# Rows s and -s in one partition block: an FFT mixing and channel-mix kernel on Trainium2

## The chip, the cores and the metric

The kernel runs on one core of a Trainium2 chip. The metric is the device time of one execution in microseconds (us). A core has engines that run side by side, each with a queue of its own in program order: TensorE (PE in the profile; PEld is its weight load), VectorE (DVE), ScalarE (ACT), GpSimd (POOL) and SyncE (SP). POOL also issues the loads that convert float32 to float16, SP the stores.

## The reference

```python
X = np.fft.fft(np.fft.fft(x, axis=1), axis=2).real     # x: 8 x 3072 x 256, float32
X_prev = X shifted by one row along axis 1, zeros first
xk = mu_k * X + (1 - mu_k) * X_prev
xr = mu_r * X + (1 - mu_r) * X_prev
k = np.maximum(xk @ w_k, 0)                             # 256 -> 1024
v = (k * k) @ w_v                                       # 1024 -> 256
out = 1 / (1 + np.exp(-(xr @ w_r))) * v                 # float32
```

## The kernel before

An image is one of the 8 batch entries. The FFT over 3072 rows is split as 48 x 64: row n = 64 n1 + s, with n1 from 0 to 47 and s from 0 to 63. Three stages of matrix products make the real part of the spectrum.

Stage A sums over n1. A load puts 96 partitions of x into SBUF as float16 (`xh`, in two halves h of 16 columns q each): partition p holds the rows 32 p to 32 p + 31, so the even partitions hold s = q and the odd ones s = q + 32. `butterfly` (line 117) adds and subtracts the two halves of the features into `eo`; then `a_item` (line 438) multiplies eight 96 x 128 blocks, as weights, with the table `w_pm` of 96 moving columns (48 parts of frequencies times the two values of s in a block). For image 0 and half of image 1, `a_sum` (line 452) works on `xh` itself, with two accumulating products of 192 columns in place of a butterfly and two of 96. `evac` (lines 424 and 426) copies PSUM to `a` in float16, on DVE ("V") or ACT.

Stage D transforms the features. For each of 24 units u, the weights are a 128 x 128 block of `a` (the real and the imaginary part of a frequency times 64 values of s) and the moving matrix is `w_eo` of 128 columns, 64 cosine and 64 sine; e = 0 and 1 are the even and odd features (`d_units`, line 462). Four units make a `d_item`, evacuated to `g_all` with 1024 elements a partition. Cosine and sine columns are formed for all 128 rows of a block.

Stage C sums over s. `c_item` (line 493) takes for each of 27 slots (a frequency each, from -1 to 25) two blocks of `g_all` as weights, with the tables `m1` and `m2` of 64 columns as moving matrices, into `pq`. Feature 128 doesn't fit into the 128 partitions: image 0 has a third product a slot for it, the others form it with `turned` (three small DVE products, line 509), two products at the end of the last item (line 499), a small evacuation `f` and a small store within SBUF (`flat`, line 516).

Then `halves` (line 525), `diff` and `mix` on DVE give the mixed inputs, and the main loop runs 48 chunks of 512 rows (six an image) of four steps each: `k_piece` (wk, line 589; its Relu on ACT, line 599), `square` on DVE (line 606), `r_item` (wr, line 613; Sigmoid on ACT, line 618), `v_tile` (wv, line 627) and `v_out` (line 637; stores, line 645).

The order is written by hand: `pin_order` at the end holds each engine to program order. What belongs to later images stands in a table of steps, filled by `at(step, f, ...)`: in each step PE gets a `k_piece`, then due items of A, D, C and r, then a `v_tile`. While the chunks of image b run, stages A, D and C of image b + 2 are fed in between, and DVE forms the inputs of image b + 1. PSUM tiles come from three slots of 1024 columns (`ps_w`, used by A, D, C, k and r in turn) and two of 512 (`ps_v`). The x of image b + 3 is loaded when a buffer of `xh` (two) comes free.

Ahead of the loop stands the prologue (lines 649 to 677): POOL issues the loads of image 0 and 1 and the weights' gathers, with small operations between them; DVE and ACT make the tables `w_pm`, `w_eo`, `m1` and `m2` from index patterns and sines; PE runs stage A of image 0 as x arrives, and its first D and C items. `keep_busy` multiplies zeros.

Of the kernel before, what the change touches and what calls it, by code (L numbers as in the profile page):

```python
# [17 lines left out]
MAGIC = 12582912.0  # L18
# [15 lines left out]

@with_exitstack
def kernel(
# [17 lines left out]
    GU = 386  # L54
    NS1 = 17

    const = ctx.enter_context(tc.tile_pool(name="const", bufs=1))
    xh_pool = ctx.enter_context(tc.tile_pool(name="xh", bufs=2))
# [39 lines left out]
    x_r = x.rearrange("b (p r) d -> b p r d", r=32)  # L98
    xh_t = {}
    eo_t = {}  # L100

    def load_part(b, h, q0, nq):

        nc.gpsimd.dma_start(out=xh_t[b, h][:, q0:q0 + nq],  # L104
                            in_=x_r[b, :, 16 * h + q0:16 * h + q0 + nq, :])
# [46 lines left out]
    def mu_rows(a):  # L152
        for p0, f0, step, n in (((0, 0, 1, 1), (1, 1, 2, 64), (65, 2, 2, 63)),
                                ((0, 128, 1, 1), (1, 255, -2, 64), (65, 254, -2, 63)))[a]:
            nc.scalar.activation(out=mu_p[:, a, p0:p0 + n], in_=_v(mu_row, f0, [(step, n)]),
                                 func=AF.Copy)
# [10 lines left out]
    load_part(0, 0, 0, 8)  # L167
    pcol_i = const.tile([P, 1], INT32)
    nc.gpsimd.iota(pcol_i, pattern=[[0, 1]], base=0, channel_multiplier=1)
    k1c_i = const.tile([P, 24, 2], INT32)  # L170
    nc.gpsimd.iota(k1c_i, pattern=[[1, 24], [0, 2]], base=0, channel_multiplier=0)
    load_part(0, 0, 8, 8)
    veo_i = const.tile([P, 2, 64], INT32)
    nc.gpsimd.iota(veo_i, pattern=[[-1, 2], [2, 64]], base=2, channel_multiplier=0)
# [6 lines left out]
    for c in range(2):  # L181
        nc.gpsimd.tensor_scalar(out=ueo[:, :, c], in0=veo_i, scalar1=pd_f,
                                scalar2=(0.5 + 0.25 * c) * TURN, op0=ALU.mult, op1=ALU.add)
    load_part(0, 1, 0, 4)
    load_part(0, 1, 4, 4)
    kst_i = const.tile([P, NSL + 64], INT32)
    nc.gpsimd.iota(kst_i[:, 0:NSL], pattern=[[1, NSL]], base=-1, channel_multiplier=0)
    nc.gpsimd.iota(kst_i[:, NSL:NSL + 64], pattern=[[1, 64]], base=0, channel_multiplier=0)
    load_part(0, 1, 8, 4)
    load_part(0, 1, 12, 4)  # L190
    for i in range(2):
        nc.gpsimd.tensor_scalar(out=unit[:, i:i + 1], in0=pcol_i[0:2], scalar1=float(i),
                                scalar2=None, op0=ALU.is_equal)
# [3 lines left out]

    phs = {}

    def phase(lo, hi):  # L200
        lo, hi = (lo + 0.5) % 1.0, (hi + 0.5) % 1.0
        if (lo, hi) not in phs:
# [639 lines left out]
```

## Time and profile before

| What | Value |
|---|---|
| median of 14 runs | 455.68 us (454.92 to 458.74) |
| the profiled execution | 457.67 us |
| its span | 455.8 us |
| granted TensorE clock, mean | 0.995 |
| HBM read, written | 28.84 MB, 25.17 MB |

The span is from the first to the last instruction that the profiler records; the execution's own time holds it and what lies around it. Busy times of engines overlap. In the groups of the page and in the timeline a line gives the source line, the engine and the operation, what is written from what, the shape, and how many. Matmuls are pipelined: the busy time of a product includes its way through the array, so the pace of a stage is read from one start to the next. Of the page's costliest groups, these are evacuations (A, r and D):

```profile
L426 ACT ACTIVATE a<-psW 128x768 f16<-128x768 f32 x61 | 49.1, 808 | 3.3 <-PE psW L452 3.3
L618 ACT ACTIVATE r<-psW 128x1024 f16<-128x1024 f32 x48 | 49.0, 1020 | 0.8 <-PE psW L613 0.8
L426 ACT ACTIVATE g_all<-psW 128x1024 f16<-128x1024 f32 (+1 forms) x47 | 47.9, 1027 | 0.0
```

After the bar stand the busy time in us, the mean of one in ns, and, after the second bar, how long the engine stood idle ahead of them and for what.

### The profile page before, as it was taken

The numbers are of one execution on the slowest core, as the hardware profiler recorded it, in microseconds if no ns is written. First come the engines' busy times: TensorE is split into PE (matmuls) and PEld (weight loads), VectorE is DVE, ScalarE is ACT, GpSimd is POOL, SyncE is SP. The second block draws the span as 40 slices with busy tenths as digits, with TensorE's granted clock in tenths as the row PEclk, the third lists the DMA queues.
The fourth block names the chain that finished last, engine by engine and source line by source line (L and its number), as shares of the span: only waits on it lengthen the run. The fifth ranks groups of instructions, "written<-read, shape, count | busy, mean of one in ns | idle before, by whom it ended". The sixth has DMA issues, their size and how long they took to land.

```text
span 455.8 us, 9755 instructions
## 1 busy us (share of the span) xinstructions
PE 445.5 (98%) x4082; PEld 327.7 (72%) x4082; DVE 356.0 (78%) x495; ACT 361.6 (79%) x413; POOL 38.8 (9%) x72
## 2 busy tenths in 40 slices
PE   6999999999999999999999999999999999999995
PEld 3767777777777777777777777777777777666764
DVE  7799879986797868877789777888779755997453
ACT  6899998788788888888887888788878888666661
POOL 5858100000000000000000000000000000000000
PEclk9899999999999999999999999999999999999999
DMA  7865861627521473125622265222222121222223
GB/s 133 123 127 106 181 137 44 132 65 139 118 70 48 81 153 92 47 70 113 142 48 70 61 127 120 66 71 47 71 48 70 46 71 47 71 70 70 70 69 94
DMA packets 32524, 40.25 MB, mean 88 GB/s; under 512 B 3838, under 2 KB 29952, under 8 KB 31232
## 3 DMA queue, kind: packets, MB, share of 16 engines
q1 hardware_dynamic: 27776, 25.07, 21.9%
q0 software_dynamic: 4544, 14.42, 18.7%
q8 instruction: 32, 0.52, 0.5%
q10 hardware_dynamic: 160, 0.13, 0.1%
q14 instruction: 12, 0.10, 0.1%
HBM read 28.84 MB, written 25.17 MB: 118 GB/s over the span
## 4 chain that ended last, share of the span: by engine, by line
PE 93%; ACT 3%; DMA 2%; DVE 1%; issue 1%; POOL 0%; POOLq 0%
PE psV L627 36%; PE psW L589 35%; PE psW L613 9%; PE psW L462 4%; PE psW L438 4%; PE psW L493 3%; DMA xh<-in_x_dram 2%; ACT rl L599 1%; PE psW L452 1%; ACT g_all L426 0%; DVE x L569 0%; ACT L618 0%; ACT a L426 0%; ACT r L618 0%; DVE y L525 0%
## 5 line engine op out<-in xcount | busy, mean ns | idle before, releaser
L599 ACT ACTIVATE rl<-psW 128x1024 f16<-128x1024 f32 x192 | 196.3, 1025 | 79.7 <-PE psW L589 79.4
L627 PE MATMUL psV<-wv_sb,k 128*128 128x256 f16 x1536 | 198.7, 273 | 0.0
L589 PE MATMUL psW<-x,wk 128*128 128x512 f16 (+1 forms) x776 | 196.7, 377 | 0.3 <-ACT rl L599 0.3
L606 DVE TENSOR_TENSOR k<-rl 128x2048 f16<-128x2048 f16 (+1 forms) x98 | 117.5, 1201 | 61.3 <-ACT rl L599 60.6
L627 PEld LDWEIGHTS <-k 128*128 128x128 f16 x1536 | 143.5, 98 | 20.2
L589 PEld LDWEIGHTS <-wk 128*128 128x128 f16 x776 | 75.7, 98 | 50.4 <-issue 0.4
L637 DVE SCALAR_TENSOR_TENSOR o<-psV,r 128x512 f32<-128x512 f32 (+1 forms) x97 | 66.2, 683 | 23.7 <-PE psV L627 21.7
L558 DVE TENSOR_TENSOR x<-y,t 128x1536 f16<-128x1536 f16 x60 | 57.5, 958 | 2.1
L426 ACT ACTIVATE a<-psW 128x768 f16<-128x768 f32 x61 | 49.1, 808 | 3.3 <-PE psW L452 3.3
L613 PE MATMUL psW<-wr,x 128*128 128x256 f16 x384 | 49.8, 273 | 0.0
L618 ACT ACTIVATE r<-psW 128x1024 f16<-128x1024 f32 x48 | 49.0, 1020 | 0.8 <-PE psW L613 0.8
L613 PEld LDWEIGHTS <-x 128*128 128x128 f16 x384 | 37.5, 98 | 14.4
L426 ACT ACTIVATE g_all<-psW 128x1024 f16<-128x1024 f32 (+1 forms) x47 | 47.9, 1027 | 0.0
L117 DVE TENSOR_TENSOR eo<-xh 96x2048 f16<-96x2048 f16 x26 | 31.5, 1213 | 1.6 <-DMA xh<-in_x_dram 1.6
L462 PEld LDWEIGHTS <-a 128*128 128x128 f16 x384 | 25.0, 98 | 10.2 <-issue 0.6
L438 PEld LDWEIGHTS <-eo 96*128 96x128 f16 x416 | 23.4, 97 | 11.6
L104 POOL DMA_DIRECT2D xh<-in_x_dram x21 | 11.2, 537 | 226.0 <-DVE eo L117 221.7
L426 ACT ACTIVATE pq<-psW 128x896 f16<-128x896 f32 (+5 forms) x34 | 28.8, 851 | 0.4 <-PE psW L493 0.3
L462 PE MATMUL psW<-w_eo,a 128*128 128x128 f16 x376 | 28.4, 219 | 0.3 <-ACT rl L599 0.3
L438 PE MATMUL psW<-w_pm,eo 96*128 96x96 f16 x416 | 26.3, 206 | 0.0
L493 PEld LDWEIGHTS <-g_all 128*128 128x128 f16 x459 | 17.8, 98 | 8.3 <-ACT g_all L426 1.7
L493 PE MATMUL psW<-m,g_all 128*128 128x64 f16 x442 | 19.2, 194 | 0.8 <-ACT g_all L426 0.7
(107 smaller groups left out, 171.9 us busy)
## 6 DMA issues: line engine op xcount, KB each, us to landing
out_dram<-o SPq DMA_DIRECT2D x190, 128.0 KB, 2.4
xh<-in_x_dram POOLq DMA_DIRECT2D x13, 768.0 KB, 6.8
xh<-in_x_dram POOLq DMA_DIRECT2D x4, 384.0 KB, 5.8
xh<-in_x_dram POOLq DMA_DIRECT2D x4, 192.0 KB, 6.5
wv_sb<-in_moe_w_v_dram POOLq DMA_DIRECT2D x1, 512.0 KB, 8.3
out_dram<-o ACTq DMA_DIRECT2D x2, 64.0 KB, 2.0
out_dram<-o SPq DMA_DIRECT2D x2, 64.0 KB
y<-f SPq DMA_DIRECT2D x7, 3.4 KB
```

Of the source, the lines that this page charges most:

```text
L426: nc.scalar.activation(out=out_ap, in_=in_ap, func=AF.Copy)
L438: nc.tensor.matmul(out=ps[:, 128 * i:128 * i + 96], lhsT=eo[:, 8 * j + i, e, :], rhs=w_pm[0:96, 0], start=True, stop=True)
L462: nc.tensor.matmul(out=_v(ps, 256 * i + 64 * (1 - e), [(128, 2), (1, 64)]), lhsT=a_t[b][:, e, 2 * u:2 * u + 2, :], rhs=w_eo[:, e, :], star ...
L493: nc.tensor.matmul(out=ps[:, o + 64 * i:o + 64 * i + 64], lhsT=g_all[:, u, col:col + 128], rhs=m[:, sl] if sl != 1 else mz[:, 0 if m is m1 ...
L558: V.tensor_tensor(out=dst, in0=_v(y_t[b], 64 * (NSL * a + lo + 3 * m), [(1, n)]), in1=_v(x_t["t", a], 64 * lo, [(1, n)]), op=ALU.subtract ...
L589: nc.tensor.matmul(out=st["k", ds][:, 512 * hs + lo:512 * hs + hi], lhsT=wk_sb[m][a][:, 128 * fc:128 * fc + 128], rhs=xk[:, a, 512 * i + l ...
L599: nc.scalar.activation(out=st["rl"][:, 2 * ds:2 * ds + 2], in_=st["k", ds].rearrange("p (f t) -> p f t", f=2), func=AF.Relu, bias=0.0, sca ...
L606: V.tensor_tensor(out=k2_t[c][:, lo:hi], in0=r, in1=r, op=ALU.mult)
L613: nc.tensor.matmul(out=ps[:, 256 * tb:256 * tb + 256], lhsT=x_t[b, 1, m][:, a, 512 * i + 128 * tb: 512 * i + 128 * tb + 128], rhs=wr_sb[m] ...
L618: nc.scalar.activation(out=st["r", c], in_=ps, func=AF.Sigmoid)
L627: nc.tensor.matmul(out=st["v", tb - h][:, 256 * h:256 * h + 256], lhsT=k2_t[c][:, fc, 128 * tb:128 * tb + 128], rhs=wv_sb[:, fc], start=(f ...
L637: V.scalar_tensor_tensor(out=o.rearrange("p a b -> p (a b)")[:, 0:256 * n], in0=st["v", t0][:, 0:256 * n], scalar=16.0, in1=st["r", c][:, ...
```

## The change

The two rows that share a partition block are now s and -s (modulo 64) instead of s and s + 32: `load_rows` loads 48 partitions with rows 64 n1 + q, and 48 others with rows 64 n1 + 64 - q, in descending order, so that stage A's own sum over the 96 partitions gives the even part in s (`part` 0) and the odd part (`part` 1) at once. `w_pm` then has 104 columns (two parts, 26 frequencies, two values), in two versions, as the block q = 0 holds rows 0 and 32. Stage D takes the cosine features from the even part and the sine features from the odd part alone: four products of 63 to 65 columns for a pair of frequencies, 13 pairs an image, in four items (4, 4, 4 and 1 pairs). Feature 128 is one of the cosine columns, so `turned`, `flat`, `u128` and their tables are gone. `g_all` holds the pairs; stage C multiplies a pair's block with one table `m_c`, whose rows for the other frequency of the pair are zero. `halves` turns the sign of one row of `pq` first. The prologue's table computations are rewritten, `xh` has three buffers instead of two, and each load of x is two DMAs, or three where it holds the block q = 0.

```diff
     NSL = 27
-    GU = 386
-    NS1 = 17
+    NU = 26
+    NJ, NJ1 = 14, 9
     const = ctx.enter_context(tc.tile_pool(name="const", bufs=1))
-    xh_pool = ctx.enter_context(tc.tile_pool(name="xh", bufs=2))
+    xh_pool = ctx.enter_context(tc.tile_pool(name="xh", bufs=3))
...
-    x_r = x.rearrange("b (p r) d -> b p r d", r=32)
...
+    def load_rows(b, h, g, q0, nq):
+        q = 16 * h + q0
+        r = (64 - q if q else 32) if g else q
+        src = dataclasses.replace(x[b, r:r + 1, :],
+                                  ap=[[64 * D, N1], [-D if g else D, nq], [1, D]])
+        nc.gpsimd.dma_start(out=xh_t[b, h][48 * g:48 * g + 48, q0:q0 + nq], in_=src)
     def load_part(b, h, q0, nq):
-        nc.gpsimd.dma_start(out=xh_t[b, h][:, q0:q0 + nq],
-                            in_=x_r[b, :, 16 * h + q0:16 * h + q0 + nq, :])
+        load_rows(b, h, 0, q0, nq)
+        if h == 0 and q0 == 0:
+            load_rows(b, h, 1, 1, nq - 1)
+            load_rows(b, h, 1, 0, 1)
+        else:
+            load_rows(b, h, 1, q0, nq)
...
+    g_all = const.tile([P, NU // 2, 256], FP16)
+    m_c = const.tile([P, 2 * NJ, 64], FP16)
+    mn = const.tile([P, 64], FP16)
+    V.memset(m_c, 0.0)
+    V.memset(mn, 0.0)
+    warm = const.tile([P, 1], FP32)
+    nc.scalar.activation(out=warm, in_=zeros[:, 0:1], func=AF.Sin, bias=0.0, scale=1.0)
...
+    w_pm = const.tile([P, 2, 3, 4 * NU], FP16)
...
+    ts(one["t"], one["p"], -2.0, MUL, 47.0 * TURN / 48.0, ADD)
+    ts(one["n"], one["t"], one["g"], MUL, one["p"], ADD)
+    ts(one["o0"], one["g"], 0.5 * TURN, MUL, 0.5 * TURN, ADD)
+    ts(one["o1"], one["g"], 0.5 * TURN, MUL, 0.75 * TURN, ADD)
+    for part, c, ph in ((0, 0, 0.75 * TURN), (0, 1, 0.0), (1, 0, one["o0"]), (1, 1, one["o1"])):
+        ts(u_w[:, 0, part, :, c], k1c_i, one["n"], MUL, ph, ADD)
...
+    u_f = u_w.rearrange("p t a k c -> p (t a k c)")
+    ts(u_f, u_f, TURN - 1, ALU.bitwise_and)
+    nc.scalar.activation(out=w_pm[:, :, 0:2],
+                         in_=_v(u_f, 0, [(4 * NU, 2), (0, 2), (1, 4 * NU)]), func=AF.Sin,
+                         bias=m_pi, scale=TWO_PI / TURN)
+    nc.scalar.activation(out=w_pm[:, :, 2], in_=_v(u_f, 0, [(4 * NU, 2), (1, 4 * NU)]),
+                         func=AF.Sin, bias=p_pi, scale=-TWO_PI / TURN)
...
-    m1 = const.tile([P, NSL, 64], FP16)
-    m2 = const.tile([P, NSL, 64], FP16)
...
+    def m_sine(j0, j1):
+        for part, odd in ((hi64, 0), (lo64, 1)):
+            nc.scalar.activation(
+                out=m_c.rearrange("p (j o) t -> p j o t", o=2)[part, j0:j1, odd],
+                in_=ang[part, j0:j1], func=AF.Sin, bias=m_pi[part], scale=TWO_PI / TURN)
+    def m_first():
+        im = slice(96, 128)
+        nc.scalar.activation(out=m_c[im, 0], in_=m_c[im, 0], func=AF.Copy, scale=row["sgn"][im])
+        V.memset(m_c[hi64, 0, 0:1], 0.0)
+        nc.scalar.activation(out=mn[hi64], in_=m_c[hi64, 0], func=AF.Copy, scale=-1.0)
...
-            nc.tensor.matmul(out=ps[:, 128 * i:128 * i + 96], lhsT=eo[:, 8 * j + i, e, :],
-                             rhs=w_pm[0:96, 0], start=True, stop=True)
-        evac(_v(a_t[b], 3072 * e + 2 * (16 * h + 8 * j), [(64, 48), (2, 8), (1, 2)]),
-             _v(ps, 0, [(2, 48), (128, 8), (1, 2)]), eng)
+            nc.tensor.matmul(out=ps[:, 128 * i:128 * i + 4 * NU], lhsT=eo[:, 8 * j + i, e, :],
+                             rhs=w_pm[0:96, int(h + j + i == 0), 0], start=True, stop=True)
+        evac(_v(a_t[b], 128 * NU * e + 16 * h + 8 * j, [(32, 4 * NU), (1, 8)]),
+             _v(ps, 0, [(1, 4 * NU), (128, 8)]), eng)
...
-                nc.tensor.matmul(out=ps[:, 256 * i:256 * i + 192],
+                nc.tensor.matmul(out=ps[:, 256 * i:256 * i + 8 * NU],
                                  lhsT=xh[:, q0 + i, 128 * k:128 * k + 128],
-                                 rhs=w_pm[0:96, k:k + 2], start=(k == 0), stop=(k == 1))
-        evac(_v(a_t[b], 2 * (16 * h + q0), [(64, 96), (2, n), (1, 2)]),
-             _v(ps, 0, [(2, 96), (256, n), (1, 2)]), eng)
-    def d_units(b, ps, u0, n):
+                                 rhs=w_pm[0:96, int(h + q0 + i == 0), k:k + 2],
+                                 start=(k == 0), stop=(k == 1))
+        evac(_v(a_t[b], 16 * h + q0, [(32, 8 * NU), (1, n)]),
+             _v(ps, 0, [(1, 8 * NU), (256, n)]), eng)
+    def d_units(b, ps, u0, n, bank):
         for i in range(n):
-            u = u0 + i
-            for e in range(2):
-                nc.tensor.matmul(out=_v(ps, 256 * i + 64 * (1 - e), [(128, 2), (1, 64)]),
-                                 lhsT=a_t[b][:, e, 2 * u:2 * u + 2, :],
-                                 rhs=w_eo[:, e, :], start=True, stop=True)
+            for e, part, c0, c1 in ((0, 0, 0, 65), (0, 1, 65, 128), (1, 0, 0, 64), (1, 1, 64, 128)):
+                o = bank * e + 128 * i
+                nc.tensor.matmul(out=ps[:, o + c0:o + c1],
+                                 lhsT=a_t[b][:, e, part, 2 * (u0 + i):2 * (u0 + i) + 2, :],
+                                 rhs=w_eo[:, e, c0:c1], start=True, stop=True)
+    def d_evac(ps, u0, n, bank, eng):
+        evac(_v(g_all, 256 * u0, [(64, 2), (128, 2 * n), (1, 64)]),
+             _v(ps, 0, [(bank, 2), (64, 2 * n), (1, 64)]), eng)
     def d_item(b, n, eng="A"):
+        k = min(4, NU // 2 - 4 * n)
         ps = ps_w()
-        d_units(b, ps, 4 * n, 4)
-        evac(g_all[:, 4 * n:4 * n + 4, 1:257], ps.rearrange("p (i c) -> p i c", c=256), eng)
+        d_units(b, ps, 4 * n, k, 512)
+        d_evac(ps, 4 * n, k, 512, eng)
...
+        d_units(b, ps, u, 2, 256)
+        d_evac(ps, u, 2, 256, eng)
...
-            u = {-1: 1, 24: 0, 25: 23}.get(sl - 1, sl - 1)
-            for o, col, m, first, last in ((0, 128, m1, True, True), (512, 0, m2, True, b > 0),
-                                           (512, 256, m1, False, True))[:2 if b else 3]:
+            u = max(sl - 1, 1 - sl)
+            for o, col in ((0, 0), (512, 128)):
                 nc.tensor.matmul(out=ps[:, o + 64 * i:o + 64 * i + 64],
-                                 lhsT=g_all[:, u, col:col + 128],
-                                 rhs=m[:, sl] if sl != 1 else mz[:, 0 if m is m1 else 1],
-                                 start=first, stop=last)
-        if b and s0 + n == NSL:
-            for k in range(2):
-                nc.tensor.matmul(out=ps[:, 448:512], lhsT=u128[:, k],
-                                 rhs=(m1, m2)[k][:, 1], start=(k == 0), stop=(k == 1))
+                                 lhsT=g_all[:, u // 2, col:col + 128],
+                                 rhs=mn if o and sl == 0 else m_c[:, sl],
+                                 start=True, stop=True)
         evac(pq[:, :, s0:s0 + n, :], _v(ps, 0, [(512, 2), (64, n), (1, 64)]), eng)
-        if b and s0 + n == NSL:
-            y_t[b, "f"] = f = y_pool.tile([NSL, 64], FP16, name="f")
-            nc.scalar.activation(out=f, in_=ps[0:NSL, 448:512], func=AF.Copy)
-    def turned(b):
-        for s0, n, u0, step in ((1, 24, 0, 1), (25, 2, 0, 23), (0, 1, 1, 1)):
-            V.tensor_tensor(out=u128[:, :, s0:s0 + n],
-                            in0=_v(g_all, GU * u0 + 256, [(0, 2), (GU * step, n)]),
-                            in1=tw[:, :, s0:s0 + n], op=ALU.mult)
-    def flat(b):
-        V.memset(y_t[b, "f"][0:1, 0:1], 0.0)
-        nc.sync.dma_start(out=y_t[b][0:1, 1], in_=y_t[b, "f"])
...
+        if (lo, hs[0]) == (0, 0):
+            V.tensor_scalar(out=pq[0:1, 1, 0], in0=pq[0:1, 1, 0], scalar1=-1.0, scalar2=None,
+                            op0=ALU.mult)
...
-    m_sine(0, NS1)
+    m_sine(0, NJ1)
+    m_first()
     a_sum(0, 0, 8, "V")
     a_sum(0, 0, 12)
-    m_angles(NS1, 22)
-    m_swap(0, NS1)
+    m_angles(NJ1, NJ)
     a_sum(0, 1, 0, "V")
     a_sum(0, 1, 4)
-    m_zero()
     a_sum(0, 1, 8)
     a_sum(0, 1, 12, "V", 2)
     a_sum(0, 1, 14, "A", 2)
-    m_angles(22, NSL)
-    m_ends()
     mu_turn()
     d_half(0, 0, ps_v(), "A")
     d_half(0, 2, ps_v(), "V")
-    d_half(0, 4, ps_w(), "A")
-    d_half(0, 6, ps_w(), "V")
-    m_wrap(NS1, NSL)
+    m_wrap(NJ1, NJ)
     c_item(0, 0, 5)
     c_item(0, 5, 4)
-    d_item(0, 2)
-    d_item(0, 3)
+    d_item(0, 1)
...
-    at(4, m_swap, NS1, NSL)
-    at(4, m_last)
     at(4, loads_2)
-    at(4, d_item, 0, 4)
-    at(4, d_item, 0, 5)
+    at(4, d_item, 0, 2)
+    at(4, d_item, 0, 3)
...
-    for n, st0 in enumerate((13, 14, 14, 15, 16, 17)):
+    for n, st0 in enumerate((13, 14, 15, 17)):
         at(st0, d_item, 1, n)
...
-            for n, st0 in enumerate((29, 30, 31, 34, 35, 38)):
+            for n, st0 in enumerate((29, 31, 34, 38)):
                 at(s0 + st0, d_item, t, n)
-            at(s0 + 39, turned, t)
...
-            at(s0 + (18 if b else 20), flat, t)
...
```

## The prediction

> **What bounds the kernel now.** I read the page's first two blocks, then the chain that ended last, then busy time by stretches, then single stages of the timeline.
>
> ```profile
> span 455.8 us, 9755 instructions
> PE 445.5 (98%) x4082; PEld 327.7 (72%) x4082; DVE 356.0 (78%) x495; ACT 361.6 (79%) x413; POOL 38.8 (9%) x72
> ...
> PE 93%; ACT 3%; DMA 2%; DVE 1%; issue 1%; POOL 0%; POOLq 0%
> ```
>
> PE is busy almost everywhere and carries 93% of the chain. But a busy PE need not stream at its peak, so the stretches come next: per line the stretch, its sum, then PE, PEld, DVE, ACT, POOL, the granted clock and DMA.
>
> ```profile
> 22.00:56.00 34.00, 33.17 (x323) 24.64 (x321) 31.41 (x48) 31.36 (x37) 18.23 (x28) 1.00 0.73 133
> 56.00:110.00 54.00, 54.00 (x537) 40.37 (x534) 45.45 (x58) 46.62 (x53) 1.52 (x3) 1.00 0.51 110
> 110.00:164.00 54.00, 54.00 (x506) 39.88 (x505) 43.30 (x55) 44.44 (x50) 1.01 (x2) 1.00 0.40 88
> ```
>
> From 56 us on PE has no gap in a stretch of 54 us (about one image), the clock is full, and ACT has 9.6 us to spare. The starts of groups in the timeline give the pace of each stage (start, busy, engine, line):
>
> ```profile
> 138.25 0.51 PE L438 MATMUL psW<-w_pm,eo 96*128 96x96 f16 x8
> ...
> 138.59 1.04 PE L627 MATMUL psV<-wv_sb,k 128*128 128x256 f16 x8
> ...
> 139.46 1.03 PE L589 MATMUL psW<-x,wk 128*128 128x512 f16 x4
> ...
> 142.94 0.61 PE L462 MATMUL psW<-w_eo,a 128*128 128x128 f16 x8
> ...
> 143.38 1.04 PE L627 MATMUL psV<-wv_sb,k 128*128 128x256 f16 x8
> ...
> 161.22 0.57 PE L493 MATMUL psW<-m,g_all 128*128 128x64 f16 x14
> ...
> 161.62 1.04 PE L627 MATMUL psV<-wv_sb,k 128*128 128x256 f16 x8
> ```
>
> From one start to the next: 0.34 us for 8 products of 96 columns is 42.5 ns each (stage A); 0.44 for 8 of 128 is 55 (stage D); 0.40 for 14 of 64 is 29 (stage C, each with weights of its own); 0.87 for 8 of 256 is 109. So a product costs about 0.416 ns per moving column ((109 - 42.5)/160) plus some 2.5 ns, down to 64 columns, and the weight load stays behind it. An image's DFT stages are then 64 x 42.5 + 48 x 55 + 56 x 29 = 2.72 + 2.64 + 1.62 = 7.0 us of its 54. These columns are what the change touches, and no wait stands between them and the end.
>
> The start is another regime:
>
> ```profile
> 4.52 0.46 DVE L267 TENSOR_TENSOR w_pm<-t,w_sg 128x288 f16<-128x288 f32 x1
> ...
> 5.69 1.49 PE L452 MATMUL psW<-w_pm,xh 96*128 96x192 f16 x16 [0.89 <-DMA xh<-in_x_dram]
> ...
> 9.55 5.13 PE L452 MATMUL psW<-w_pm,xh 96*128 96x192 f16 x40 [2.14 <-DMA xh<-in_x_dram]
> ...
> 17.53 1.26 POOL L377 DMA_DIRECT2D wv_sb<-in_moe_w_v_dram  x1
> ...
> 21.20 4.74 PE L589 MATMUL psW<-x,wk 128*128 128x256 f16 x28
> 21.52 3.94 PEld L589 LDWEIGHTS <-wk 128*128 128x128 f16 x27 [0.24 <-DMA wk<-in_moe_w_k_dram,row_i]
> ```
>
> Stage A waits twice for x; its table w_pm is ready at 4.98, 0.7 us before the first x. The main loop begins at 21.2, when the mixed x, the weights wk and the last stage C group come together.
>
> **What the Trainium skill says.** "TensorE: Matmul & The Clock Gate", section "Back-to-back issue gap", gives N/2.4 + 2.5 ns warm for one product, but about 81 ns at N=128 for a stream with a weight load before each. The trace agrees with the first (55 at 128, 29 at 64) and not with the second; I use the trace. The same page, "LDWEIGHTS (loading the stationary operand)", puts 128 columns at 107 ns; the trace records 98 ns per load, but fourteen loads and products pass in 0.40 us, so loads overlap and 29 ns is the pace. "ScalarE: Activation LUTs", section "What ACT_TABLE_LOAD costs": 186 ns + 0.833 ns per element, 93 more for a pointer bias. Against 826 and 1039 computed, the trace has 805 for 768 elements and 1028 for 1024: agreed. "DMA: Bandwidth & Descriptors", "Why small descriptors are slow (HBM only)": some 3 cycles on top of one per 32 bytes, so 9% for 1 KB as my estimate; no row of before isolates it.
>
> **The change part by part.**
>
> *Stage A, images 2 to 7.* 64 products grow from 96 to 104 columns: 64 x 8 x 0.416 = +0.21 us. Image 1 has 32 of its products as sums with 192 columns going to 208: +0.21 for these, +0.11 for the others.
>
> *Stage D.* 48 products of 128 columns (2.64 us) become 13 x 4 = 52 of 63 to 65 (52 x 29 = 1.51 us): -1.13 us an image. Fewer columns are streamed although there are four more weight loads.
>
> *Stage C.* 56 products of 64 columns become 54: -0.06 us.
>
> Images 2 to 7: +0.21 - 1.13 - 0.06 = -0.98 each, -5.9. Image 1: +0.32 - 1.19 = -0.87. All of it lies where PE has no gap, so it comes off the end one for one: -6.8 us. What is late next there is still PE.
>
> *Image 0 inside the loop.* 16 products of 128 columns become 20 of 64 (0.88 to 0.58), and ten slots of stage C lose a third product each (10 x 29): -0.6 us. Near there (22 to 30) ACT is busy without gap too, and it loses as much: two evacuations of 1.0 us become 1.0 and about 0.4. I count -0.6; ends 0 and -0.8.
>
> *ACT, DVE and SP in the loop.* Evacuating A is 832 elements instead of 768, +0.05 x 8; D is three of 1.03 and one of 0.4 instead of six, -2.7; the column f, -0.2. DVE loses three products and a memset (0.244 + 0.161 + 0.158 + 0.06) and gains one 64-element row, about 0.15 (bounds 0.06, the memset, and 0.2). SP loses one small store an image. None is on the path: nothing. What it would cost if the read pattern of A's evacuation, single elements 512 bytes apart instead of pairs, were slow is rival 3.
>
> *x loads.* Each load is split in two or three, and the mirrored rows go in 1 KB pieces. Issue on POOL: 0.54 us for a plain one, and wv (1024 pieces of that size) took 1.26, so 16 mirrored rows on 48 partitions (768 pieces) cost 1.06. In the loop POOL has over 50 us per image and waits for buffers: nothing. While wv was under way, at 23 to 26 us, the DMA moved 190 to 214 GB/s, as with plain loads (186 to 197), so I take a mirrored half at up to 9% slower: image 0 is 3.1 MB, read at about 390 GB/s (twice the written 195) in 8 us, its half slower by 0.4 us.
>
> *The prologue, step by step.* DVE: between the copy of the partition index (2.25) and w_pm stand now 21 instructions, nine of which wait for the one ahead. Waiting ones follow at 0.22 (3.04, 3.32, 3.56, 3.79), others at 0.07 (six starts from 3.96 to 4.33): 2.25 + 9 x 0.22 + 12 x 0.07 = 5.1, +0.27 for the last; then two sines on ACT (0.28 + 416 x 0.833 = 0.63 and 0.45) instead of the product: w_pm at 6.4 instead of 4.98 (bounds 5.7 and 7.2). POOL: three DMAs instead of one fill the first eight rows, the last issued at about 3.5; they land at about 5.7 to 6.2. So the first sums start at 6.4, +0.7. They are 1.6 us long and the next x was not there before 9.55, which covers it. That next x is issued at 5.2 instead of 2.3 and in two, but needs only its own 2 us of DMA time: 9.3 to 10. The last x of image 0 is issued by 9.7 instead of 6.6 and lands at 12.5 to 14; its sums ran at 14.5. Queued behind the two sines of the stage C table (0.76 each instead of 1.20 together) on ACT are the memset on DVE that waits for the sign copy, and behind it the third evacuation: at about 11.4 instead of 10.42. Together: stage A of image 0 ends 0.3 to 1 us later. Against it stand half the D products before the loop, one D evacuation of 1.0 us on ACT less, two on DVE/ACT of 0.6 and 0.7 less, and the weights wk, issued earlier since the third buffer of xh frees POOL from its 3.4 us wait: second gather at 15.6 instead of 16.46. I take the loop's start at +0.3 us, bounds -1 and +3.
>
> Sum: -6.8 - 0.6 + 0.3 = -7.1 us. Against the profiled execution, 457.67 us with a span of 455.8: span 448.7, time 450.6. That execution lies 2.0 us above the median 455.68, so the forecast for the median is **448.6 us**.
>
> **The rivals.**
>
> 1. *The prologue eats part of it.* For: PE is fed by DMA until 10 us; the table chain is 1.4 us later; after a longer gap the clock may be at half for longer (stretch 12 to 14 shows 0.50). Against: x was the later one, and evacuations get fewer. With the start 4 us late: 455.7 - 7.4 + 4 = 452.3.
> 2. *The prologue gains.* The chain from 16 to 21 us runs through evacuations, of which about 2 us vanish. If x keeps up, 446 us or somewhat less.
> 3. *Slower: ACT becomes the bound in stage A.* If reading single elements 512 bytes apart takes two cycles each, an evacuation takes 0.17 + 832 x 1.667 = 1.56 us. In the ten steps of the loop that hold the eight A groups, ACT needs 10 x 1.025 + 2 x 1.02 + 8 x 1.56 = 24.8, PE 10 x 1.74 + 2 x 0.87 + 8 x 0.366 = 22.1. Less one evacuation of lead (0.9), PE stalls 1.8 us an image, some 12 in all: 460.5. It decides from 1.46 us per evacuation on, where the stall equals the 1.0 us gained. Against: pairs 512 bytes apart cost the same per element as contiguous reads (805 for 768, 1028 for 1024).
> 4. *D does not speed up*, because a product cannot go below 55 ns with new weights: 52 x 55 = 2.86, each image +0.37, so 455.7 + 2.6 + 0.3 = 458.6; break-even at 48 ns. Against: stage C passes at 29 ns under the same conditions.
>
> That the change doesn't cut the columns isn't open: the counts of products follow from the code.
>
> **How the numbers follow.** Forecast 0.76; rival 1 0.12; rival 2 0.05; rival 3 0.04; rival 4 0.03. The forecast's bounds: -6.8 certain within 0.5, image 0 between 0 and -0.8, start between -1 and +3: 455.7 - 9.1 and 455.7 - 3.8; both ends at once are unlikely, so 446.4 to 451.4, which leaves out rivals 1, 3, 4 and part of 2. A measurement of this kernel can tell about 0.2% (0.9 us) from no change. Faster: 0.76 + 0.11 + 0.05 = 0.92; same: 0.01 from rival 1 and 0.01 from 4; slower: 0.04 + 0.02.
>
> **What would show it.** Right: eight A products in 0.37 us, a D group of 16 in 0.46, PE without gap from 56 us on, ACT's share down by some 2.5 us an image; the first product of the main loop at 20 to 24 us. Wrong: D groups of 16 in 0.8 us or more; A evacuations well over 0.86 us with PE waiting for them; x of image 0 landing after 15 us; a loop that starts after 25 us.

## The result, and the profile after

The changed kernel takes 452.94 us (median of 10 runs, 451.12 to 454.88), the kernel before beside it 455.89 (47 runs, 454.92 to 458.74): a ratio of 0.9928, with a 95% interval of 0.9913 to 0.9942. It is faster by 3.0 us, where the prediction had 7.1. Its profiled execution took 453.68 us.

The page of the changed kernel, as its counterpart in the prediction:

```profile
span 451.9 us, 9677 instructions
...
PE 441.0 (98%) x4073; PEld 321.8 (71%) x4073; DVE 352.4 (78%) x472; ACT 344.9 (76%) x390; POOL 43.4 (10%) x78
...
PE 93%; ACT 3%; POOL 1%; DMA 1%; issue 0%; DVE 0%; POOLq 0%
...
L387 ACT ACTIVATE a<-psW 128x832 f16<-128x832 f32 x61 | 52.2, 860 | 3.8 <-PE psW L413 3.8
```

The shares look as before: PE is still the bound. The stretches of the changed kernel (start, sum, then PE, PEld, DVE, ACT, POOL, granted clock, DMA share, GB/s) show where to look:

```profile
22.00:56.00 34.00, 33.06 (x318) 23.82 (x316) 32.37 (x54) 31.27 (x38) 11.15 (x15) 0.95 0.96 161
56.00:110.00 54.00, 54.00 (x564) 40.35 (x563) 45.45 (x56) 44.81 (x50) 4.40 (x7) 1.00 0.52 97
110.00:164.00 54.00, 54.00 (x516) 39.41 (x515) 43.99 (x52) 42.92 (x48) 3.11 (x5) 1.00 0.48 94
```

From 56 us on there is no gap on PE and the clock is full; ahead of that the clock is 0.95 where it was 1.00. In the timeline of the changed kernel the starts give the paces of A, D and C:

```profile
121.60 0.53 PE L399 MATMUL psW<-w_pm,eo 96*128 96x104 f16 x8
121.97 1.04 PE L576 MATMUL psV<-wv_sb,k 128*128 128x256 f16 x8
...
144.17 0.64 PE L427 MATMUL psW<-w_eo,a 128*128 128x65 f16 x16
144.65 1.04 PE L576 MATMUL psV<-wv_sb,k 128*128 128x256 f16 x8
...
161.65 0.57 PE L457 MATMUL psW<-m_c,g_all 128*128 128x64 f16 x14
162.06 1.04 PE L576 MATMUL psV<-wv_sb,k 128*128 128x256 f16 x8
```

Eight A products in 0.37 us, sixteen of D in 0.48 (30 ns each), fourteen of C in 0.41. So the loop does what was forecast. The first products of `r_item`, in the kernel before and in the changed kernel:

```profile
32.28 0.49 PE L613 MATMUL psW<-wr,x 128*128 128x256 f16 x3
35.43 0.49 PE L562 MATMUL psW<-wr,x 128*128 128x256 f16 x3
```

From there to the end of the span it was 455.8 - 32.28 = 423.5 us before and is 451.9 - 35.43 = 416.5 now: 7.0 us less. The start gives back about half of it. The timeline of the changed kernel there:

```profile
6.73 1.59 PE L413 MATMUL psW<-w_pm,xh 96*128 96x208 f16 x16 [1.33 <-DMA xh<-in_x_dram]
6.78 4.08 POOL L112 DMA_DIRECT2D xh<-in_x_dram  x7
9.80 1.59 PE L413 MATMUL psW<-w_pm,xh 96*128 96x208 f16 x16 [1.26 <-DMA xh<-in_x_dram]
12.96 4.32 PE L413 MATMUL psW<-w_pm,xh 96*128 96x208 f16 x24 [1.58 <-DMA xh<-in_x_dram]
...
18.60 1.01 PE L176 MATMUL psW<-unit,mu_p 2*128 2x2 f32 x4
...
24.89 4.96 PE L538 MATMUL psW<-x,wk 128*128 128x256 f16 x28
```

Image 0's x comes in four parts of eight columns q. Stage A now waits for the first three of them, for the third until 12.96, where the kernel before waited for the first two. The main loop begins at 24.89 instead of 21.20: 3.69 us later. Then the granted clock (the third figure from the end; 0.50 is half of the full clock), first of the changed kernel:

```profile
10.00:12.00 2.00, 1.39 (x16) 1.14 (x13) 0.55 (x2) 1.77 (x5) 1.59 (x5) 1.00 1.19 173
12.00:14.00 2.00, 1.04 (x7) 0.92 (x8) 0.96 (x2) 0.66 (x1) 1.42 (x3) 0.52 1.07 154
...
18.00:20.00 2.00, 2.00 (x17) 1.63 (x16) 0.76 (x2) 0.70 (x2) 1.47 (x2) 0.50 0.76 108
...
24.00:26.00 2.00, 2.00 (x23) 1.59 (x24) 1.97 (x6) 1.37 (x3) 1.70 (x2) 0.57 1.34 218
```

and of the kernel before:

```profile
10.00:12.00 2.00, 2.00 (x20) 1.91 (x18) 1.55 (x3) 0.81 (x1) 0.56 (x1) 0.71 0.86 159
12.00:14.00 2.00, 2.00 (x15) 1.83 (x14) 1.64 (x5) 0.29 (x1) 1.41 (x5) 0.50 0.76 98
14.00:16.00 2.00, 1.91 (x19) 1.65 (x18) 0.96 (x3) 1.98 (x6) 1.78 (x5) 0.94 0.77 141
```

Before, the half clock lasted from about 11 to 14 us. Now it lasts from 12 to about 25.7, over the sums of the last two parts of x and over D and C of image 0. The 32 sums from 12.96 on take 5.64 us, until 18.60, the first start behind them: 176 ns each, where the 16 from 6.73 to 8.15 took 89 each at the full clock. For the same two parts the kernel before took 4.36 us, from 10.90 to 15.26.

Last, the queue on which POOL's loads run (packets, MB, share of 16 engines' span), before:

```profile
q0 software_dynamic: 4544, 14.42, 18.7%
```

and in the changed kernel:

```profile
q0 software_dynamic: 16128, 14.42, 22.3%
```

The same bytes in 3.5 times as many packets, and 0.223 x 451.9 - 0.187 x 455.8 = 15.5 us more of all sixteen DMA engines, for eight images: 1.9 us an image.

So two theories stood for the start. **Loads:** image 0's x, in nine DMAs instead of six and half of it in 1 KB pieces, comes later and in more portions, and PE's waits bring the half clock with them. **Tables:** the rewritten table computations on DVE and ACT hold up the first sums and the evacuations. A third, **clock**, has the half clock as a cause of its own, apart from the loads.

### The profile page after: what moved, and what is told of

The parts are those of the page before. It is cut to its first block, busy times and chain, and to the rows that moved or that the text cites. A ratio compares the mean times of both kernels' runs of the same rounds, so it can differ in the third digit from the quotient of the medians.

```text
span 451.9 us, 9677 instructions
## 1 busy us (share of the span) xinstructions
PE 441.0 (98%) x4073; PEld 321.8 (71%) x4073; DVE 352.4 (78%) x472; ACT 344.9 (76%) x390; POOL 43.4 (10%) x78
## 3 DMA queue, kind: packets, MB, share of 16 engines
q0 software_dynamic: 16128, 14.42, 22.3%
## 4 chain that ended last, share of the span: by engine, by line
PE 93%; ACT 3%; POOL 1%; DMA 1%; issue 0%; DVE 0%; POOLq 0%
PE psV L576 37%; PE psW L538 36%; PE psW L562 9%; PE psW L399 4%; PE psW L457 3%; PE psW L427 3%; PE psW L413 1%; ACT rl L548 1%; DMA xh<-in_x_dram 1%; POOL xh L112 1%; ACT g_all L387 0%; PE psV L413 0%; ACT L567 0%; ACT m_c L330 0%; ACT pq L387 0%
## 5 line engine op out<-in xcount | busy, mean ns | idle before, releaser
L387 ACT ACTIVATE a<-psW 128x832 f16<-128x832 f32 x61 | 52.2, 860 | 3.8 <-PE psW L413 3.8
L112 POOL DMA_DIRECT2D xh<-in_x_dram x46 | 28.7, 631 | 216.0 <-DVE eo L132 215.1
L399 PEld LDWEIGHTS <-eo 96*128 96x128 f16 x416 | 24.4, 97 | 11.6
L399 PE MATMUL psW<-w_pm,eo 96*128 96x104 f16 x416 | 27.7, 209 | 0.0
L387 ACT ACTIVATE g_all<-psW 128x1024 f16<-128x1024 f32 (+1 forms) x31 | 26.4, 858 | 0.1
L427 PEld LDWEIGHTS <-a 128*128 128x128 f16 x416 | 17.3, 100 | 7.1 <-issue 0.5
L494 DVE TENSOR_SCALAR t<-d,mu_m 128x1536 f16<-128x1536 f16 x32 | 19.6, 614 | 0.0
L474 DVE TENSOR_TENSOR y<-pq 128x896 f16<-128x896 f16 (+5 forms) x38 | 18.6, 532 | 1.1 <-ACT pq L387 0.8
```

The costliest lines, as they stand in the source:

```text
L112: nc.gpsimd.dma_start(out=xh_t[b, h][48 * g:48 * g + 48, q0:q0 + nq], in_=src)
L387: nc.scalar.activation(out=out_ap, in_=in_ap, func=AF.Copy)
L399: nc.tensor.matmul(out=ps[:, 128 * i:128 * i + 4 * NU], lhsT=eo[:, 8 * j + i, e, :], rhs=w_pm[0:96, int(h + j + i == 0), 0], start=True, s ...
```

## The experiments

### The loads alone

**e6** puts the changed kernel's loads into the kernel before, with its two buffers; image 0 and the others then hold rows in another order than the old tables expect.

```diff
 (kernel before; load_rows and load_part as in the changed kernel)
...
-    load_part(0, 0, 0, 8)
+    load_rows(0, 0, 0, 0, 8)
...
-    load_part(0, 0, 8, 8)
+    load_rows(0, 0, 1, 1, 7)
+    load_rows(0, 0, 1, 0, 1)
...
-    load_part(0, 1, 0, 4)
-    load_part(0, 1, 4, 4)
+    load_part(0, 0, 8, 8)
...
-    load_part(0, 1, 8, 4)
-    load_part(0, 1, 12, 4)
+    load_part(0, 1, 0, 8)
+    load_part(0, 1, 8, 8)
```

> The kernel before with the changed kernel's loads of x (split, mirrored, in the changed kernel's places on POOL), two buffers, all else as it was (the rows do not fit its stage A, so the content is another). Theory: the form of the loads costs some 3 us by itself, and the kernel before gets slower by 2 to 4 us, 458 to 460, its loop starting at 23 to 25 instead of 21.2. Rival (the loads only hurt together with the changed kernel's longer table chain and its third buffer): within 1 us of before, 455 to 456.7.

Measured: 461.21 us, ratio 1.0098 (1.0066 to 1.013) to the kernel before. Its timeline has the first product of the loop at 25.39:

```profile
9.98 6.69 PE L464 MATMUL psW<-w_pm,xh 96*128 96x192 f16 x40 [1.32 <-DMA xh<-in_x_dram]
...
25.39 0.82 PE L601 MATMUL psW<-x,wk 128*128 128x256 f16 x6
```

The loop of the old tables and the old stages starts 4.2 us later with nothing but the new loads. That is more than the forecast had (458 to 460 us, a start at 23 to 25); the half clock lies from about 9 to 23 us here. The second part of x comes only 0.43 us later than before (9.98 instead of 9.55) and no later part is waited for; from there the sums take 7.89 us instead of 5.71, and D and C up to the loop 7.52 instead of 5.94. So in this profile most of the 4.2 us goes by at half clock, and a shorter wait (1.32 us, where the kernel before had 2.14) stands ahead of it. The form and the places of the loads are enough to cause the late start, by the waits or by the clock that follows: neither the new tables nor the third buffer of `xh` is needed for it.

**e4** goes the other way: the changed kernel with image 0's x in four plain loads of 96 partitions (the content of image 0 differs).

```diff
 (changed kernel)
...
+        if b == 0:
+            nc.gpsimd.dma_start(out=xh_t[b, h][:, q0:q0 + nq],
+                                in_=x_r[b, :, 16 * h + q0:16 * h + q0 + nq, :])
+            return
...
-    load_rows(0, 0, 0, 0, 8)
+    load_part(0, 0, 0, 8)
...
-    load_rows(0, 0, 1, 1, 7)
-    load_rows(0, 0, 1, 0, 1)
```

> The changed kernel with image 0's x loaded in whole 96-partition DMAs, four instead of nine, rows in the order of the kernel before (image 0's rows s and -s are not paired, so the content of image 0 is another). Theory 2b (splitting and mirroring costs POOL and DMA time): the waits end at 5.7, about 9 and 11, as before the change, and the loop starts at 21 to 22.5, 449 to 450.5. Theory 3 or 1 alone: x still lands after 12.5 or PE is still at half clock until 25 us, 452 to 453.

Measured: 449.81 us, ratio 0.9869 (0.9838 to 0.99), 3.1 us below the changed kernel; the loop starts at 22.24. Both lie inside what was expected of this run, and the time is within 1.2 us of the prediction's 448.6. PE still waits 1.86 us for the third part of x, until 12.00 where about 11 was expected:

```profile
12.00 3.97 PE L417 MATMUL psW<-w_pm,xh 96*128 96x208 f16 x24 [1.86 <-DMA xh<-in_x_dram]
...
22.24 4.11 PE L542 MATMUL psW<-x,wk 128*128 128x256 f16 x25 [0.49 <-DVE x L522]
```

**e5** keeps the nine DMAs and their places, but reads the second 48 partitions in one contiguous piece each (content differs), and **e10** keeps e4's four loads, but with eight descending rows a partition, so that all of image 0's x goes in 1 KB pieces (content differs).

```diff
 (e5; the rest of the call is brought into the new shape)
-        r = (64 - q if q else 32) if g else q
+        r = 32 + q if g else q
-                                  ap=[[64 * D, N1], [-D if g else D, nq], [1, D]])
+                                  ap=[[64 * D, N1], [1, nq * D]])
...
 (e10, against e4)
-                                in_=x_r[b, :, 16 * h + q0:16 * h + q0 + nq, :])
+                                in_=dataclasses.replace(
+                                    x[b, 16 * h + q0 + nq - 1:16 * h + q0 + nq, :],
+                                    ap=[[32 * D, 96], [-D, nq], [1, D]]))
```

> The changed kernel with the same DMAs, but the second 48 partitions of every load take rows 64 n1 + 32 + q in ascending order, one contiguous piece of up to 16 KB a partition instead of pieces of 1 KB (rows s and -s are not paired, so the content is another). Theory A (the 1 KB pieces are slow, or cost POOL more): most of the 3 us that whole loads gave come back, the third wait ends at about 12 or before, the loop starts at 22 to 23, 449.5 to 451. Theory B (the number of DMAs and POOL's time for them): no better than the changed kernel by more than 0.7 us, 452.3 to 453.5.

> The kernel of e4 (image 0's x in four loads of all 96 partitions), but each partition's eight rows read in descending order, so that all of image 0's x goes in pieces of 1 KB; content of image 0 differs, as its rows stand in another order than the tables expect. If the number of separate loads and their issue on POOL is what delays x (theory of number), the time stays at e4's 449.8 within 0.5. If the small pieces are what delays x (theory of pieces), twice as many of them as in the changed kernel cost at least what the changed kernel lost: 452.5 or more, with the last x of image 0 landing after 12.8 us.

Measured: e5 452.21 us (0.9895, 0.9856 to 0.9934), e10 453.81 (0.9962, 0.9941 to 0.9983). So, as the theory of pieces had it, with four loads small pieces for the whole image cost 4.0 us (e10 against e4), and the sums of the third part start at 12.81 instead of 12.00:

```profile
12.81 4.34 PE L419 MATMUL psW<-w_pm,xh 96*128 96x208 f16 x24 [0.77 <-DMA xh<-in_x_dram]
...
24.00 2.31 PE L544 MATMUL psW<-x,wk 128*128 128x256 f16 x17 [0.50 <-DVE x L524]
```

Small pieces take POOL longer to issue (0.77 to 0.91 us a load, where e4's four took 0.51 to 0.65) and the DMA longer to move (22.7% against 21.8% on the queue); which of the two delays the sums isn't separated, and the half clock is longer too (10.2 us against 3.4).

What the number and the spacing of the loads cost, e5 doesn't tell. Its median lies 2.4 us above e4's, between the two theories' ranges, but its interval overlaps e4's and the changed kernel's, and its profiled execution (451.21 us), its fastest, has the third part's sums at 11.70 and the loop at 22.31, about as e4. The queue of e5 shows that as many DMAs with large pieces take no more DMA time than in the kernel before (18.7%):

```profile
q0 software_dynamic: 5136, 14.42, 18.8%
```

### One cure at a time

Four kernels each mend one thing in the changed kernel.

```diff
 (e1: products of zeros fill PE's waits)
     a_sum(0, 0, 4)
-    keep_busy(1)
+    keep_busy(7)
...
     a_sum(0, 0, 12)
+    keep_busy(8)
 (e2: two buffers for x, so that image 1's loads don't follow at once)
-    xh_pool = ctx.enter_context(tc.tile_pool(name="xh", bufs=3))
+    xh_pool = ctx.enter_context(tc.tile_pool(name="xh", bufs=2))
 (e3: all of image 0's x ahead of POOL's small operations)
     load_rows(0, 0, 1, 0, 1)
+    load_part(0, 0, 8, 8)
+    load_part(0, 1, 0, 8)
+    load_part(0, 1, 8, 8)
...
-    load_part(0, 0, 8, 8)
...
-    load_part(0, 1, 0, 8)
-    load_part(0, 1, 8, 8)
 (e7: wk's gathers ahead of image 1's first x)
-        load_part(1, 0, 0, 8)
         for a in range(2):
             next(row_part)
             gather(wk_sb[0][a], moe_w_k, a)
+        load_part(1, 0, 0, 8)
```

> The changed kernel with six more products of zeros after the second sum of image 0 (1.3 us at full clock) and eight after the fourth (1.7 us), in the two waits for x. Theory 1 (clock): the main loop of the changed kernel starts 3.7 us late because PE idles from 8.5 to 9.8 and from 11.4 to 13.0 and then runs at half clock until 25.4; kept busy, the clock stays full, the last sums of image 0 take 2.8 us less, the loop starts at about 21.5 instead of 24.9, and the time falls by 2.5 to 4 us to about 449.5. Theory 2 (x arrives late, the clock is a bystander that ACT or DVE hide): clock full, but the loop starts less than 1 us earlier, 452 to 453.

> The changed kernel with two buffers of x as before, so that POOL cannot issue image 1's first x (three DMAs from 8.8 to 10.9) before the first sums have freed a buffer. Theory 3 (the third buffer lets image 1's x take DMA time from image 0's last x): the third wait of the sums, which ended at 12.96, ends at about 11.5 to 12, the loop starts 1 to 2 us earlier. Theories 1 and 2: the wait ends within 0.4 us of where it did, the loop starts no earlier or, as the weights are issued later, up to 1 us later: 453 to 454.

> The changed kernel with all DMAs of image 0 issued ahead of POOL's other small operations (veo, pd, ueo, kst). Theory 2 (POOL issues x too late): the second wait ends at about 8.5 instead of 9.80 and the third at about 11 instead of 12.96, PE is idle less, and the loop starts 2 to 3 us earlier unless the stage C table, whose index patterns now come at about 9 us, is late (then the same as the changed kernel, with ACT and DVE waiting for it). Theory 1 alone: the loop's start follows the clock; with waits shorter than the changed kernel's the half clock should be shorter too, so the start and the granted clock move together.

> The changed kernel with the two gathers of wk issued ahead of the first x of image 1, three buffers. Theory 3 refined (image 1's x competes with image 0's last x, and two buffers cured that but delayed wk): the third wait ends at about 11 to 11.5 instead of 12.96, wk is there before it is needed, and the loop starts 1 to 2 us earlier: 451 to 452. Rival: the order doesn't matter, since the DMA has room: 452.5 to 453.2.

| kernel | median us | ratio to before (95%) | loop's first product | what PE waits for then |
|---|---|---|---|---|
| changed | 452.94 | 0.9928 (0.9913 to 0.9942) | 24.89 | x, three times |
| e1 | 452.74 | 0.9927 (0.9901 to 0.9953) | 23.05 | its first sums, at half pace, and its own fillers, until 11.26 and 14.41 |
| e2 | 452.89 | 0.9922 (0.9895 to 0.9948) | 22.23 | wk, 1.37 us, behind the first product, until 23.86 |
| e3 | 454.36 | 0.9961 (0.9945 to 0.9976) | 23.29 | an evacuation on DVE, 1.32 us |
| e7 | 453.73 | 0.9926 (0.9895 to 0.9957) | 23.90 | an evacuation on ACT, 2.75 us |

None of the four moves the median down by more than 0.2 us, and e3 is slower than the changed kernel by 1.4 us (their intervals don't overlap). In none of them does PE stand for the third part of x any more; in e2 and e7 that is in part because the sums ahead of it ran at half clock and came to it only at 13.21 and 12.29. In each, something else holds PE then. In e2's timeline it is wk, whose gathers stand behind POOL's wait for a buffer, so that the early first product of the loop brings the first `r_item` only 0.4 us forward (35.03 instead of 35.43). The loop's start moved further than its third theory had it (1 to 2 us), and the time didn't move:

```profile
10.48 5.43 PE L413 MATMUL psW<-w_pm,xh 96*128 96x208 f16 x40 [0.98 <-DMA xh<-in_x_dram]
...
23.86 2.39 PE L538 MATMUL psW<-x,wk 128*128 128x256 f16 x12 [1.37 <-DMA wk<-in_moe_w_k_dram,row_i]
```

In e3 the sums run without a break from 10.01 (at half pace, 173 ns each, until 13.47), and then stand for a PSUM tile. On DVE the memset of the stage C table waited from 12.13 to 14.16 for ACT's sign copy, with the evacuation behind it in the queue; the table is later because POOL's small operations, its inputs, are:

```profile
15.32 1.59 PE L413 MATMUL psW<-w_pm,xh 96*128 96x208 f16 x16 [1.32 <-DVE a L385]
```

The theory of the tables is right about this: they are next in line. In e7, which came out above what either of its theories had (451 to 452 and 452.5 to 453.2), PE stands 2.75 us for an evacuation that ACT starts late; ACT itself was idle for 1.64 us ahead of it, with a releaser that the profile can't name. A like idle time (1.00 to 1.62 us) is in e5, e8 and e9. What it is stays open.

e1 was to keep the clock full, and doesn't isolate the clock. The record of the granted clock begins with its first entry, in e1 at 10.10 us, and a stretch ahead of that prints 1.00; but there the first sixteen sums run at half pace, 173 ns each where the changed kernel took 89:

```profile
6.66 2.93 PE L413 MATMUL psW<-w_pm,xh 96*128 96x208 f16 x16 [1.23 <-DMA xh<-in_x_dram]
```

From 10.10 on the clock was full, and the profiled execution (451.71 us) starts the loop 1.8 us earlier than the changed kernel's. But the slow first sums and the fillers behind them hold back x that is already there (11.26 instead of 9.80), and the median gains nothing. How much the half clock costs apart from the waits, no run shows.

### Several cures together

**e8** is e7 with image 0's second x ahead of the feature table on POOL and three and two fillers. **e9** joins e3's and e7's orders and moves the stage C table behind evacuations on ACT. **e11** is e9 with one evacuation more on DVE and the sign copy last. **e12** is e11 with six fillers more.

```diff
 (e8, against e7)
     load_rows(0, 0, 1, 0, 1)
+    load_part(0, 0, 8, 8)
...
-    load_part(0, 0, 8, 8)
...
-    keep_busy(1)
+    keep_busy(3)
...
     a_sum(0, 0, 12)
+    keep_busy(2)
 (e9, beside the orders of e3 and e7)
-    m_sine(0, NJ1)
-    m_first()
     a_sum(0, 0, 8, "V")
     a_sum(0, 0, 12)
+    m_sine(0, NJ1)
     m_angles(NJ1, NJ)
     a_sum(0, 1, 0, "V")
+    m_first()
 (e11, against e9)
-    m_first()
     a_sum(0, 1, 4)
-    a_sum(0, 1, 8)
+    a_sum(0, 1, 8, "V")
...
     a_sum(0, 1, 14, "A", 2)
+    m_first()
 (e12, against e11)
-    keep_busy(10)
+    keep_busy(14)
...
-    keep_busy(1)
+    keep_busy(3)
```

> As the one with the weights first, and in addition image 0's second x (two DMAs) ahead of POOL's feature table, and two and two more products of zeros in the waits of the first sums. If the start's delay is x (issue and competition) plus the half clock, this starts the loop at 22 to 22.5 with the clock full: 449 to 450.5. If the table chain on DVE and ACT (third evacuation at 11.5) is what holds the sums, it is no better than the one with the weights first.

> The changed kernel with all of image 0's x issued ahead of POOL's small operations (as in e3), the weights' gathers ahead of image 1's x (as in e7), and on ACT the sines and the sign copy of the stage C table moved behind the evacuation of the fourth group of sums and the memset behind the fifth, so that no evacuation of stage A waits for the table. If the start is lost to a row of waits of which each stands behind the next (x, the table, the weights), then with all three moved the sums run without a gap from about 10 us to 15 or 16, the main loop starts at 20.5 to 22 instead of 24.9, and the time is 449 to 450.5. If instead the number of loads and the DMA's own rate set the start, x stays late, and the time stays within 0.2% of 452.9.

> The kernel of e9 with one evacuation more on VectorE (the seventh group of sums) and the sign copy of the stage C table behind the last evacuation. In e9 the first products of stage D waited 1.56 us for an evacuation on ACT that stood behind the table, and the granted clock went to half soon after that gap. If that wait set the start, D begins at 16 instead of 17.4, no gap of over 0.7 us is left between the sums and the loop's first product but for ACT's evacuations, the loop starts at 21 to 22.3 instead of 23.6, and the time is 450.0 to 452.0. If the half clock comes from the first 10 us (the wait of 1.84 us at 7 us), the time stays within 0.2% of e9's 453.2.

> The kernel of e11 with four more products of zeros ahead of the first sums and two more behind the first two groups, so that TensorE has no gap of over 1 us before the loop. If the wait and the half clock after it are what the start still loses, the clock stays full up to the loop, the loop starts at 20.5 to 22, and the time is 449 to 450.7, which is at or below e8's 450.7, the fastest so far that computes the reference. If the order of the loads is what matters and the clock is not, the time is that of e11 within 0.2%, or more by the fillers' own time.

| kernel | median us | ratio to before (95%) | loop's first product |
|---|---|---|---|
| e8 | 450.71 | 0.9854 (0.9816 to 0.9892) | 22.91 |
| e9 | 453.24 | 0.994 (0.9923 to 0.9957) | 23.60 |
| e11 | 451.78 | 0.9904 (0.9886 to 0.9921) | 23.48 |
| e12 | 450.39 | 0.988 (0.9865 to 0.9896) | 22.88 |

e9 missed its range. Its sums did run from 9.09 without a break of over 0.3 us, but then D stood for an evacuation on ACT behind the moved table, and soon after this wait the clock fell to half until about 25 us. The timeline of e9:

```profile
15.25 0.60 PE L176 MATMUL psW<-unit,mu_p 2*128 2x2 f32 x4
17.41 0.65 PE L427 MATMUL psV<-w_eo,a 128*128 128x65 f16 x16 [1.56 <-ACT a L387]
...
23.60 2.62 PE L538 MATMUL psW<-x,wk 128*128 128x256 f16 x14
```

e11 takes that wait down to 0.46 us and the median by 1.5 us, as expected of the time. The path was not the expected one: D began at 18.47 and the loop at 23.48, where 16 and 21 to 22.3 were forecast, so the time came right by luck. In that profile the second part of x came at 9.98 instead of 9.09 and the half clock lay in the first sums. e12's fillers take another 1.4 us. The time is inside its range, the loop's start (22.88) is not (20.5 to 22). In its stretches the half clock is short again:

```profile
12.00:14.00 2.00, 1.68 (x12) 1.53 (x13) 1.71 (x4) 1.95 (x3) 1.43 (x5) 0.65 1.14 152
14.00:16.00 2.00, 2.00 (x13) 1.75 (x12) 0.70 (x1) 1.29 (x2) 1.99 (x4) 0.50 0.68 98
```

e8 and e12 are the fastest that compute the reference: 2.2 and 2.5 us below the changed kernel, about 5 us below the kernel before of the same runs. Their intervals overlap, so neither is ahead of the other. e8's median and start lie just outside what was expected (449 to 450.5 us, 22 to 22.5). Beside e5 to e8 a quarter of the kernel before's executions were 2 to 4 us longer than the rest, so the ratios of these four lie up to 0.4% below those of the medians (e8: 0.9854 against 0.9894).

## Why the prediction was right in direction and wrong in size

**Right: the columns.** D was to cost 29 ns a product and took 30, A's group of eight 0.37 us and took it, C 29 and took 29. The steady part was to give -6.8 and gave -7.0 (first `r_item` to the end). Image 0 in the loop was to give -0.6; from the loop's first product to the first `r_item` it was 32.28 - 21.20 = 11.08 us and is 35.43 - 24.89 = 10.54: -0.54. From the first `r_item` of one image to that of the next it was 53.98 us and is 53.01, the -0.98 that was forecast. Over that period ACT's busy time fell by 2.2 us (44.42 to 42.23), not quite 2.5, and the longer evacuations of A cost nothing. Rivals 3 and 4 fell at once: A's evacuation took 860 ns, far from the 1.46 us at which it would decide, and D 30 ns, below 48.

**Wrong: "I take the loop's start at +0.3 us, bounds -1 and +3".** It was +3.69. That is in effect rival 1, which stood at 452.3 with a chance of 0.12. In the profiled executions the 3.69 us divide so: the sums of the third part of x begin 2.06 us later (12.96 instead of 10.90), the sums of the last two parts take 1.28 us longer (5.64 instead of 4.36), and 0.35 us come from there to the loop. The prediction's own steps:

- w_pm was to be ready at 6.4 and was at 6.37. The third evacuation, due at 11.4, began at 11.51. The second wk gather, due at 15.6, began at 15.16. The second part of x, due at 9.3 to 10, came at 9.80. These steps held.
- "its half slower by 0.4 us", from 9% for 1 KB pieces, an estimate from the fixed 3 cycles a packet that the Trainium skill gives ("DMA: Bandwidth & Descriptors", "Why small descriptors are slow (HBM only)"). The queue lines give 1.9 us of all sixteen engines for an image's mirrored half. Plain loads took about 0.187 x 455.8 = 85 us for 14.42 MB, so some 4.6 us, as an estimate, for the 0.79 MB that half an image writes: 1.9 on 4.6 is about 40%, not 9%. The trace doesn't agree with that price here, and the measurement decides. The page's 9% was taken as the only value, with no higher bound beside it.
- The third part of image 0's x was left out. The prediction follows the second part and the last, which "is issued by 9.7 instead of 6.6 and lands at 12.5 to 14; its sums ran at 14.5", and says nothing of the one between. That one was issued from 6.78 to 7.96 instead of 4.29 to 5.36 and landed at 12.83. PE was through with the second part at about 11.4 and stood for it until 12.96; in the kernel before its sums began at 10.90 without a wait. The last part, the one that was followed, wasn't waited for. This is the step that failed: each part of a load has a reader of its own, and one of four had no term in the sum.
- The half clock was named in rival 1 and then given no price in the forecast. The 32 sums at 176 instead of 89 ns carry some 2.8 us of it, but the kernel before lost about 1.7 us in the same sums (half of its 3.4 us of half clock). So, as an estimate, about 1.1 of the 3.69 us is the longer half clock in the sums, and its part in D and C comes on top. No run isolates it, and it may weigh more than the waits: in e6 most of the delay went by at half clock.

**Mis-sized: the step to the median.** The forecast took 2.0 us off for the distance of the profiled execution from the median. The changed kernel's profiled execution lies only 0.74 above its median, so the profiled executions differ by 4.0 us (457.67 - 453.68) and the medians by 3.0. From the first `r_item` to the end the profiles hardly differ: 423.5 us in the kernel before and in e6, 416.3 to 416.5 in all twelve of the changed kernel and its variants. So, as far as the profiles show, executions differ in the start, and the 2.0 us were a late start of the profiled execution before, which the change doesn't have to share.

Shown by runs: that the loads' form and places cost the start (e6 makes the kernel before 1.0% slower with nothing else, e4 takes 3.1 us back), and that small pieces for the whole image count by themselves (e10 against e4). Not shown: how the cost divides between POOL's issue, the DMA's work and the half clock, what the number and the spacing of the loads do, and what ACT's idle time in e5, e7, e8 and e9 is.

## What to carry to other kernels

Work that streams fewer columns on a PE without gaps could be priced here from the paces of the profile to some per cent. The start could not, because there x, tables, evacuations and weights stand close behind each other and four cures, each taken alone, brought no gain. Follow every part of a load to its own reader before calling a later landing hidden, and not the last part alone. And a load in small pieces or in many parts belongs where it has a long lead: here the steady part shows no loss to the mirrored loads, while image 0's cost about 3 us (e4). Whether a plain layout with tables that fit it pays for image 0, no run shows, since e4 computes other content there.

## What the hardware showed

Two short waits were followed by a long half clock. In the changed kernel PE was idle for 1.26 us and then 1.58 us ahead of 9.80 and 12.96, and the granted clock stayed at 0.50 until about 25 us, although the record has PE busy for 2.00 of 2.00 us in each stretch from 14 to 20. The Trainium skill ("TensorE: Matmul & The Clock Gate", Part 1) has the full rate come back after at least one window of sustained activity, about 3.4 us. From the stretches of 2 us (a mean of 0.71 is 1.16 us at half) the half clock lasted 1.16 + 2 + 0.24 = 3.4 us in the kernel before and 1.4 + 2 = 3.4 in e12, which agrees; but 1.92 + 10 + 1.72 = 13.6 us in the changed kernel, and 1.32 + 4 + 1.52 = 6.8 in e9. These are four times and twice 3.4, and e10's 10.2 us are three times. So in these profiles the length goes in steps of the page's window, and one window wasn't always enough; why some go by without releasing the clock, no run here shows.

The same kernel's executions differ in the granted clock, in some kernels in step with the time: e4 took 448.95 to 449.9 us in the four executions at 0.998 or 0.999 and 452.6 at 0.986. In others they don't: the changed kernel took 452.25 and 454.88 us with 1.000 recorded and 451.12 with 0.990. That the record lacks what lies ahead of its first entry may be a reason; it isn't shown. For a change in the start, where PE has gaps, the median of several executions says more than the one that was profiled.
